# A recurrent attention with a top-2 mixture of experts on one core: products of two units on GpSimd beside the first solve, zeros and copies on other engines, gathers placed one by one

## The chip, the core and the metric

One core of a Trainium2 chip runs the whole program. The metric is the device time of one execution in microseconds (us); the median of the runs counts. The engines are TensorE (PE, with its weight loads PEld), VectorE (DVE), ScalarE (ACT), GpSimd (POOL) and SyncE (SP, which issues most DMAs). All run side by side, each takes its own instructions in order, and they wait for each other by semaphores.

## What is computed

```python
for t in range(S):                      # batch 4, 8 heads, S = 768, head size 40
    y[:, :, t] = einsum('bhd,bhde->bhe', rt, state)
    Sa = einsum('bhde,bhe->bhd', state, at)
    state = state*wt - outer(Sa, bt) + outer(vt, kt)
x = y as 3072 rows of 320
noisy = x @ w_gate + log1p(exp(x @ w_noise)) * noise      # 8 experts
top2, weights = softmax over the two largest
out[row] += weight * (relu(x[row] @ w1[e]) @ w2[e])       # for both experts of a row
```

## The kernel before

The recurrence is cut into 24 units of 64 steps (`NU`, `C`). A unit needs decays (a logarithm, a running sum by matmul, two exponentials), products of a and kb with these decays, a triangular 64x64 system for each of 32 heads, and then a chain of matmuls that carries the state on. `run` writes the order of every engine out by hand, iteration n for unit n, with the decays and products of unit n+8 (`LP`) prepared on the way. The systems of four units are solved together: `xtr` transposes the lower triangles into one tile X, `solve` or (first group only) `solve16` eliminates step by step on DVE (two TENSOR_TENSORs a step, L662 and L663), and `tout` or `tout16` transposes the result back.

Ahead of the loop stands `ramp` (L812), which prepares units 0 to 7, sets all constants, and ends in `first` (L854), the chain of unit 0. The names that matter, with their lines:

- `ln`, `sm`, `ex` (L585 to L599): the decays of unit u: a logarithm on ACT, four matmuls on PE, then on ACT a square with its accumulator read (`lc`) and two exponentials, into the tiles wq and B. `gc` (L826) copies the last decays, 104x8 numbers, to the tile gam by a DVE copy.
- `aprod`, `kprod` (L604, L607): three TENSOR_TENSORs that multiply a and kb by the decays; on POOL unless an engine is given. In `ramp` units 0 to 3 run on DVE ahead of the solve; in `first` units 4 to 7 run on DVE behind it (`vprods`).
- `LS`, `LSd` (L613, L624): 32 matmuls of the products of one unit, the ACT copy of their result into the tile la, and two small ACT copies.
- `xtr(0)` (L628), `xmask16` (L647, two DVE memsets), `solve16` (L657), `tout16` (L664: three DVE transposes and two DVE memsets of 32x512).
- `consts1(i)` (L546): constants in parts, most of them POOL memsets; part 3 also writes four identities of 32x1024 on ACT (L564). `consts16` (L652): three ACT copies of identities and a scaled copy of la, which `S16a` reads.
- `S16a`, `S16b` (L672, L678): the second stage of the first solve (PE, then ACT); `TA`, `TB`, `U`, `UT`, `P`, `Y`: the chain of a unit, each PE and then ACT, DVE in `P` and `Y`. `KBT`, `AK`, `W1`, `W2`: what stands beside it.
- `warm` (L568): matmuls of zeros whose only use is activity on PE; 24 of them (`WR`) stand before the solve's result is needed.

PE, ACT, DVE, POOL and SP each take these in the order in which `ramp` and `first` write them, so an instruction that waits holds back all behind it on its engine.

The experts follow. Rows of one expert are fetched by `gather` (L308), one indirect DMA on POOL's queue for each 128 rows, through lists that SP loads (`lists`, L303), and results go back by indirect DMAs that add (`add`, L377). Part 0 of an expert is its first 384 rows (three gathers), part 1 the next 448 (four). `experts` (L428) issues part 1 of experts 0 and 1 as soon as the lists are there, and `rest` (L437) both parts of expert 2; here a planner orders the instructions by its own costs. `s.after(i, e)` ties instruction i behind e; the list p holds instructions (relus of the hidden blocks, scalings of output tiles) that `rest` uses as such places.

Of the kernel before, what the change touches and what calls it, by code (L numbers as in the profile page):

```python
# [13 lines left out]
ALU = mybir.AluOpType  # L14
# [38 lines left out]
class Moe:  # L53
# [266 lines left out]
    def trans(s,x,e,X=None,part=0):  # L320

# [6 lines left out]
    def after(s,i,e): s.tc.add_manual_dep(i.ins,e.ins.name,mybir.DependencyInfo(mybir.DependencyClass.Sync,mybir.DependencyReason.DATA),reason="place")  # L328
# [166 lines left out]
class Att:  # L495
# [50 lines left out]
    def consts1(s,i):  # L546
        nc=s.nc; G=nc.gpsimd
        if i==0:
            G.memset(s.mk32,1.0)
            for q in range(4): G.affine_select(out=s.mk32[32*q:32*q+32,0],in_=s.mk32[32*q:32*q+32,0],pattern=[[-1,32]],base=0,channel_multiplier=1,compare_op=ALU.is_gt,fill=0.0)  # L550
        if i==1:
            s.m.ident(); G.memset(s.mk,1.0)
            for b in range(2): G.affine_select(out=s.mk[64*b:64*b+64,0],in_=s.mk[64*b:64*b+64,0],pattern=[[1,64]],base=0,channel_multiplier=-1,compare_op=ALU.is_gt,fill=0.0)
            for q in range(4): G.tensor_copy(s.i32[32*q:32*q+32],s.m.idm[32*q:32*q+32,32*q:32*q+32])
        if i==2:
            for z in s.kt: G.memset(z,0.0)
            G.memset(s.fl(s.d1)[:,128:512],0.0)
            for z in s.w: G.memset(z,0.0)
            G.memset(s.iw,0.0)
        if i==3:  # L560
            for b in range(2):
                for z,o,c in ((s.dg,32,32),(s.rp,0,0)):
                    q=slice(64*b+o,64*b+o+32)
                    nc.scalar.activation(z[q,:,c:c+32],s.m.idm[q,q].rearrange("p (o x)->p o x",o=1).to_broadcast([32,32,32]),AF.Copy)  # L564
            for z in s.S+s.St: G.memset(z,0.0)
    def warm0(s,pp,k):
        for _ in range(k): s.nc.tensor.matmul(pp,s.wz,s.wz[:,0:1].to_broadcast([128,512]),start=True,stop=True)
    def warm(s,pp,k):  # L568
        z=s.fl(s.d1)
        for _ in range(k): s.nc.tensor.matmul(pp,z[:,0:128],z[:,0:512],start=True,stop=True)  # L570
# [86 lines left out]
    def solve16(s):  # L657
        V=s.nc.vector; X=s.X; ap=lambda o,*d: bass.AP(X.tensor,X.offset+o,[X.ap[0],[528,2],*d])
        for j in range(1,15):
            m=15-j  # L660
            t=s.wk.tile([128,240],F32,name="Tt",bufs=1)[:,:2*j*m].rearrange("p (b k i)->p b k i",b=2,i=m); x=ap(j+1,[32,j],[1,m])
            V.tensor_tensor(t,ap(33*j+1,[0,j],[1,m]),ap(j,[32,j],[0,m]),op=ALU.mult)  # L662
            s.hs=V.tensor_tensor(x,x,t,op=ALU.add)  # L663
    def tout16(s):  # L664
        V=s.nc.vector; X=s.X
        V.transpose(s.rp[:,:,32:64].rearrange("p k t->p t k"),X.rearrange("p s t->p t s"))
        V.transpose(s.d16[:,:,0:16].rearrange("p k s->p s k"),X[:,0:16])
        V.transpose(s.dg[:,:,16:32].rearrange("p k s->p s k"),X[:,16:32])
# [143 lines left out]
    def ramp(s):  # L812
        nc,m=s.nc,s.m; V,G=nc.vector,nc.gpsimd
        s.consts(); s.ea=None; H=s.lh
        def load(u):
            H('ga',s.a,u); H('gkb',s.kb,u)
# [9 lines left out]
        def gc(u): V.tensor_copy(s.gam[0:RF,u],s.B[u%2][0:RF,0:520].rearrange('p (j c)->p j c',c=65)[:,:,0])  # L826
# [278 lines left out]
```

## Time and profile before

| | us |
|---|---|
| runs shown | 812.16, 810.92, 804.20 |
| their median | 810.92 |
| the profiled execution | 805.83 |
| its span, first to last instruction | 804.0 |
| busy in the span: PE, DVE, ACT, POOL | 728.4, 501.4, 399.6, 339.3 |

What lies outside the span is 1.83 us. Views of one execution give the start of an instruction from the span's start, its length, its engine and line, and in brackets how long the engine had been idle and what ended that. Several instructions of a kind are merged into a row, with xN.

### The profile page before, as it was taken

To read this page: it belongs to the slowest core of one execution; us is meant where nothing else is said; L and a number is where in the kernel's file an instruction comes from. 1 tells how busy PE (TensorE), PEld (TensorE's weight loads), DVE (VectorE), ACT (ScalarE), POOL (GpSimd) and SP (SyncE) were. 2 spreads that over 40 slices of the span, in tenths; PEclk is the share of its full clock that TensorE was granted. 3 is DMA by queue.
4 is the path that set the end of the run, shared out by engine and by line. 5 is a ranking of instruction groups with operands and counts; after the bars stand their busy time and mean duration, and the time that the engine had idled before them with its cause. 6 is when DMAs were issued, how large, how long until landed. Compare 5 with 4: busy or idle time off the path is not lost.

```text
span 804.0 us, 29172 instructions
## 1 busy us (share of the span) xinstructions
PE 728.4 (91%) x12632; PEld 531.1 (66%) x12632; DVE 501.4 (62%) x1069; ACT 399.6 (50%) x873; POOL 339.3 (42%) x463
## 2 busy tenths in 40 slices
PE   6588899999989899898888798999999999999994
PEld 4377778888877777677654365657566665766662
DVE  7866667777989857845464476856565664652321
ACT  6566667677666453464431245544434534442220
POOL 9702243345377544344358515425435151513223
PEclk9779999999999999999999899999999999999998
DMA  6542345554544632352307535536445162402113
GB/s 203 175 103 69 110 134 154 152 155 148 157 141 136 181 93 74 102 158 85 110 2 172 133 85 144 115 112 128 124 110 143 27 139 87 49 5 32 23 20 39
DMA packets 67700, 87.07 MB, mean 108 GB/s; under 512 B 15640, under 2 KB 52460, under 8 KB 67564
## 3 DMA queue, kind: packets, MB, share of 16 engines
q1 hardware_dynamic: 55404, 67.98, 28.6%
q0 software_dynamic: 12160, 17.15, 12.4%
q8 instruction: 101, 1.65, 0.9%
q14 instruction: 35, 0.29, 0.1%
HBM read 63.41 MB, written 21.69 MB: 106 GB/s over the span
## 4 chain that ended last, share of the span: by engine, by line
PE 71%; DVE 12%; ACT 8%; issue 5%; POOL 2%; DMA 0%; another core or an unknown queue 0%; ACTq 0%; DVEq 0%; POOLq 0%
PE po L369 22%; PE ph L354 20%; PE py L786 3%; PE pp L770 3%; PE pt L334 2%; PE rl L801 2%; PE tb L701 2%; PE ta L691 2%; ACT la L524 2%; ACT dr L524 2%; PE sm L591 1%; DVE Tt L640 1%; PE ut L749 1%; PE pw L723 1%; PE pw L732 1%
## 5 line engine op out<-in xcount | busy, mean ns | idle before, releaser
L377 POOL DMA_INDIRECT out_dram<-y,le x45 | 74.6, 1658 | 192.5 <-ACT y L371 189.8
L354 PE MATMUL ph<-rw__68,rk 128*128 128x384 f16 (+1 forms) x512 | 97.0, 339 | 2.9 <-DVE hl L356 1.8
L354 PE MATMUL ph<-dr,la 128*128 128x448 f16 (+1 forms) x384 | 86.0, 339 | 3.0 <-issue 3.0
L369 PEld LDWEIGHTS <-rk 128*128 128x128 f16 x576 | 56.7, 100 | 36.6 <-issue 6.6
L354 PEld LDWEIGHTS <-rk 128*128 128x128 f16 x512 | 49.5, 98 | 39.4 <-issue 3.3
L371 ACT ACTIVATE y<-po,le 128x320 f32<-128x320 f32 (+1 forms) x53 | 26.6, 504 | 93.1 <-PE po L369 79.7
L182 POOL DMA_INDIRECT ls<-ent,po x48 | 50.5, 1052 | 52.9 <-ACT pm L524 31.8
L356 DVE SCALAR_TENSOR_TENSOR hl<-ph,hh 128x448 f16<-128x448 f32 x64 | 39.2, 622 | 46.0 <-ACT hh L355 45.8
L355 ACT ACTIVATE hh<-ph 128x448 f16<-128x448 f32 x64 | 34.1, 541 | 66.0 <-PE ph L354 65.9
L355 ACT ACTIVATE rk<-ph 128x384 f16<-128x384 f32 x64 | 30.9, 488 | 62.1 <-PE ph L354 43.6
L369 PEld LDWEIGHTS <-hh 128*128 128x128 f16 (+1 forms) x640 | 46.5, 103 | 18.5 <-issue 2.7
L242 DVE TENSOR_REDUCE yc<-y 128x1 f32<-128x320 f32 (+1 forms) x53 | 23.8, 456 | 55.0 <-ACT y L371 54.9
L640 DVE TENSOR_TENSOR Tt<-X__71 128x30 f32<-128x30 f32 (+9 forms) x150 | 55.7, 372 | 3.7
L354 PEld LDWEIGHTS <-la 128*128 128x128 f16 x384 | 37.2, 98 | 29.2 <-issue 3.7
L356 DVE SCALAR_TENSOR_TENSOR rk<-ph,rk 128x384 f16<-128x384 f32 x64 | 34.4, 552 | 33.7 <-ACT rk L355 24.2
L612 POOL TENSOR_TENSOR rk<-rk,B 104x512 f32<-104x512 f32 x30 | 35.5, 1183 | 42.3 <-DVE lg L805 41.3
L641 DVE TENSOR_TENSOR X__71<-X__71,Tt 128x30 f32<-128x30 f32 (+9 forms) x150 | 49.8, 332 | 5.5
L369 PE MATMUL po<-ra,rk 128*128 128x320 f16 x288 | 45.7, 305 | 2.9 <-ACT rk L355 2.4
L786 PE MATMUL py<-pm,kt 128*64 128x104 f32 (+1 forms) x768 | 40.5, 254 | 4.1 <-issue 2.7
L772 DVE TENSOR_TENSOR pm<-pp,mk 128x1024 f32<-128x1024 f32 x24 | 29.4, 1223 | 16.5 <-PE pp L770 15.8
L786 PEld LDWEIGHTS py<-pm,kt 128*64 128x64 f32 x768 | 34.7, 137 | 7.4 <-issue 4.3
L369 PE MATMUL po<-w2h,rk 128*128 128x320 f16 x192 | 34.5, 308 | 4.3 <-issue 3.1
(329 smaller groups left out, 1731.3 us busy)
## 6 DMA issues: line engine op xcount, KB each, us to landing
rk<-in_gkb_dram SPq DMA_DIRECT2D x48, 160.0 KB
w2r<-in_w_dram SPq DMA_DIRECT2D x6, 1280.0 KB
w1s<-in_w_dram SPq DMA_DIRECT2D x28, 256.0 KB
xd<-xr SPq DMA_DIRECT2D x40, 160.0 KB
w1s<-in_w_dram SPq DMA_DIRECT2D x5, 1024.0 KB
out_dram<-z SPq DMA_DIRECT2D x15, 320.0 KB
rw__68<-in_gw_dram SPq DMA_DIRECT2D x24, 160.0 KB
ra<-in_ga_dram SPq DMA_DIRECT2D x48, 80.0 KB
```

Of the source, the lines that this page charges most:

```text
L182: st=nc.gpsimd.indirect_dma_start(out=s.ls,out_offset=OFFS(ap=po[:,j,k:k+1],axis=0),in_=s.ent[:,j,k],in_offset=None)
L354: for i,(a,b) in enumerate(mm): s.hmm=nc.tensor.matmul(ph[:,:n],a,b,start=i==0,stop=i==7)
L355: s.hrelu=nc.scalar.activation(hh[:,f],ph[:,:n],AF.Relu)
L356: s.hhl=nc.vector.scalar_tensor_tensor(hl[:,f],ph[:,:n],0.0,hh[:,f],op0=ALU.max,op1=ALU.subtract)
L369: for j in range(c): nc.tensor.matmul(po[p*j:p*j+p,:d],h[:,f,r],w[:,f,d*j:d*j+d],start=k==0,stop=k==23)
L377: st=s.nc.gpsimd.indirect_dma_start(out=o[0],out_offset=OFFS(ap=o[1],axis=0),in_=o[2],in_offset=None,compute_op=ALU.add)
L524: s.ea=s.nc.scalar.activation(*a,**k)
L612: s.after((eng or s.nc.gpsimd).tensor_tensor(z,z,b1,op=ALU.mult),e)
L640: eng.tensor_tensor(t,X[:,j:j+1,j+1:].to_broadcast([128,j,m]),X[:,0:j,j:j+1].to_broadcast([128,j,m]),op=ALU.mult)
L641: s.hs=eng.tensor_tensor(X[:,0:j,j+1:],X[:,0:j,j+1:],t,op=ALU.add)
L772: nc.vector.tensor_tensor(m.rearrange("p y j x->p (y j) x")[...,0:64],pp.rearrange("p y (j t)->p (y j) t",t=64),s.mk.to_broadcast([128,16, ...
L786: nc.tensor.matmul(pp[64*y:64*y+64,b,128*hh:128*hh+n],kt[:,j,y],m[:,y,j,0:n],start=first and hh==0,stop=True,skip_group_check=True)
```

## The change

Units 4 and 5 get their products (and the copy to gam) on POOL right after their decays and ahead of `solve16`, units 6 and 7 stay on DVE behind it; `LS(4)`, `LSd(4)`, `ex(6)`, `ln(7)`, `sm(7)`, and the matmuls of `LS(5)` move ahead of the solve, and the chain in `first` is written in another order. The loads of units 5 and 6 and the zeros of the tile kt come earlier, the zeros of S, St, w and iw later. On DVE the copy to gam becomes a TENSOR_TENSOR max, and the memsets of `xmask16` become TENSOR_TENSORs of zeros. Zeros of d1 (which `warm` reads) and of dg move to ACT. `warm` runs 8 matmuls instead of 24, and 6 more are tied behind step 8 of `solve16`. In the experts the gathers of part 1 of expert 1 and of both parts of expert 2 are tied one by one to places in p.

```diff
-    def loadx(s,e,X=None,part=0):
+    def loadx(s,e,X=None,part=0,places=()):
-        s.lists(e,X,part)
-        for _ in s.gather(e,X,part): pass
+        s.lists(e,X,part); places=list(places)
+        for g in s.gather(e,X,part):
+            if places: s.after(g,places.pop(0))
...
-        r2=s.load2(1); s.loadx(0,x,1); s.loadx(1,xn,1); ll=s.hlist.ins
+        r2=s.load2(1); s.loadx(0,x,1); s.lists(1,xn,1); ll=s.hlist.ins
...
         s.trans(x[0],0,X,1); hx=s.hx3.ins; H1=s.hidden(W1,X,1,p); s.after(s.piece1(2,5),p[5])
+        for k,g in enumerate(s.gather(1,xn,1)): s.after(g,p[3+k])
...
-              xn=s.loadx(e+1); s.loadx(e+1,xn,1); ...
+              xn=s.loadx(e+1,places=p[7:10] if e==1 else ()); s.loadx(e+1,xn,1,p[10:] if e==1 else ()); ...
...
-FT,FS,FL,FU,WR,W0,WU=2,2,4,2,24,5,2
+FT,FS,FL,FU,WR,W0,WU,WJ,WQ=2,2,4,2,8,5,2,8,6
...
+    def null16(s): s.nc.scalar.activation(s.fl(s.d1)[:,128:512],s.z[:,0:1].to_broadcast([128,384]),AF.Copy)
...
-        V=s.nc.vector; V.memset(s.X[:,0:16,16:32],0.0); V.memset(s.fl(s.X)[:,0:1024:33],1.0)
+        ... V.tensor_tensor(s.X[:,0:16,16:32],z,z,op=ALU.mult); z=s.z[:,0:32]; V.tensor_tensor(s.fl(s.X)[:,0:1024:33],z,z,op=ALU.is_equal)
...
-        for b in range(2): V.memset(s.dg[64*b+32:64*b+64,:,16:32],0.0)
+        for b in range(2): s.nc.scalar.activation(s.dg[64*b+32:64*b+64,:,16:32],s.z[...]...,AF.Copy)
...
-        def gc(u): V.tensor_copy(s.gam[0:RF,u],s.B[u%2]...[:,:,0])
+        def gc(u): z=s.B[u%2]...[:,:,0]; V.tensor_tensor(s.gam[0:RF,u],z,z,op=ALU.max)
...
-        LS[3](); s.LSd(3); s.lmask(3); s.ex(4); s.ln(5); s.sm(5); gc(4); s.ex(5); s.xtr(0); gc(5)
-        s.consts1(2); gn(6); s.consts1(3); s.xmask16()
-        s.ea=None; s.lv(0); loads(5)
+        LS[3](); s.LSd(3); s.lmask(3); s.ex(4); s.ln(5); s.sm(5); s.xtr(0); s.ex(5); s.ln(6); s.sm(6)
+        def gp(u): s.aprod(u); s.kprod(u,1); s.kprod(u,0); G.tensor_copy(s.gam[0:RF,u],...)
+        gp(4); s.xmask16(); gp(5); s.KBT(0)(); s.ex(6); s.ln(7); s.consts1(3); s.consts16()
+        s.ea=None; s.lv(0)
+        a4=s.LS(4); s.W1(0); s.warm(s.p1t('wm'),WR); a4(); s.LSd(4); s.sm(7,s.p2('sm')); s.a5=s.LS(5)
...
-        gn(7,8)
+        gn(7); s.consts1(4); gn(8)
...
-        s.KBT(0)(); s.consts16(); s.ln(6); s.W1(0)
-        s.warm(s.p1t("wm"),WR)
-        s.sm(6,s.p2("sm"))
...
-        s.solve16(); s.hA=s.hs; s.tout16(); s.first()
+        s.solve16(); s.hA=s.hs
+        if WQ: s.after(s.warm(s.p1t("wm"),WQ),s.h8)
+        s.tout16(); s.first()
...
-        s.vprods(4); s.vprods(5)
-        s.S16a(0); s.S16b(0); a4=s.LS(4); s.W2(0); s.ex(6); s.TA(0); a4(); s.ln(7); a5=s.LS(5); s.TB(0); s.vprods(6)
-        s.sm(7); a5(); s.U(0); s.LSd(4); k=s.KBT(1); s.UT(0); s.ex(7)
-        a6=s.LS(6); s.LSd(5); k(); s.ln(LP)
-        s.P(0); s.vprods(7); s.S16a(1); a6(); s.LSd(6); s.AK(1); s.Y(0); a7=s.LS(7); s.S16b(1); s.sm(LP); a7(); s.LSd(7); s.ex(LP)
+        s.S16a(0); s.vprods(6); s.gcp(6); s.a5(); s.LSd(5); s.S16b(0); s.ex(7); s.vprods(7); s.gcp(7)
+        s.W2(0); s.TA(0); k=s.KBT(1); s.TB(0); a6=s.LS(6)
+        s.U(0); k(); s.ln(LP); s.UT(0); a6(); s.LSd(6); a7=s.LS(7)
+        s.P(0); s.S16a(1); a7(); s.LSd(7); s.AK(1); s.sm(LP); s.Y(0); s.ex(LP); s.S16b(1)
```

## Rows read from the trace of the kernel before

**Rows 1.** The chain that ended last, 0 to 64 us: start, us, what.

```profile
21.52 8.44 DVE gam L826
```

**Rows 2.** Timeline of DVE: start, us, engine, line, operation, out<-in, form.

```profile
6.03 0.69 DVE L606 TENSOR_TENSOR ra<-ra,rw__68 104x512 f32<-104x512 f32 x1 [1.31 <-ACT rw__68 L524]
...
21.60 8.36 DVE L630 STREAM_TRANSPOSE X__71<-la 128x1024 f32<-128x1024 f32 x1
...
31.34 0.23 DVE L662 TENSOR_TENSOR Tt<-X__71 128x72 f32<-128x72 f32 x1
...
37.92 0.21 DVE L663 TENSOR_TENSOR X__71<-X__71,Tt 128x28 f32<-128x28 f32 x1
...
42.35 1.11 DVE L669 MEMSET dr<- 32x512 f32 x2 [0.16 <-DMA rb<-in_grb_dram]
...
73.69 0.75 DVE L640 TENSOR_TENSOR Tt<-X__71 128x30 f32<-128x30 f32 x1
...
125.41 0.18 DVE L640 TENSOR_TENSOR Tt<-X__71 128x30 f32<-128x30 f32 x1
```

**Rows 3.** Timeline of POOL around the same times.

```profile
5.53 0.96 POOL L540 MEMSET rk<- 128x1024 f32 x1
...
21.30 0.94 POOL L818 MEMSET rk<- 128x1024 f32 x1
...
29.73 0.20 POOL L81 MEMSET tri<- 128x128 f16 x1
30.00 0.29 POOL L82 TENSOR_SCALAR_AFFINE_SELECT tri<-tri 128x128 f16<-128x128 f16 x1
...
73.20 1.19 POOL L606 TENSOR_TENSOR ra<-ra,rw__68 104x512 f32<-104x512 f32 x1
```

**Rows 4.** Timeline of POOL and DVE at 252.4 to 253.3 us.

```profile
252.48 0.73 POOL L798 TENSOR_TENSOR S<-S,gam 128x320 f32<-128x320 f32 x1 [0.86 <-DVE l L216]
...
252.95 0.28 DVE L220 TENSOR_TENSOR wq<-l 128x4 f32<-128x4 f32 x1
...
253.17 1.18 POOL L606 TENSOR_TENSOR ra<-ra,rw__68 104x512 f32<-104x512 f32 x1
```

**Rows 5.** Timeline of ACT.

```profile
25.18 4.25 ACT L564 ACTIVATE dr<-idm 32x1024 f32<-32x1024 f32 x4
...
30.16 1.46 ACT L655 ACTIVATE w1s<-w1s 128x512 f32<-128x512 f32 x3
...
41.67 0.28 ACT L524 ACTIVATE w1s<-sa 128x128 f32<-128x128 f32 x1 [8.24 <-PE sa L676]
...
63.94 0.70 ACT L524 ACTIVATE dr<-sb 128x128 f32<-128x128 f32 x3 [4.08 <-PE sb L683]
...
65.30 0.84 ACT L524 ACTIVATE la<-la 32x256 f32<-32x256 f32 x2
...
69.38 0.76 ACT L524 ACTIVATE dr<-ta 32x256 f32<-32x256 f32 x2
```

**Rows 6.** Timeline of PE: the matmuls of `warm`.

```profile
25.99 5.35 PE L570 MATMUL wm<-d 128*128 128x512 f16 x24
```

**Rows 7.** Busy ACT in three stretches that hold ex(6), LS(4), ln(7) and LSd(4).

```profile
sum 3.47, ACT 3.40; mean ACT 1.13
```

**Rows 8.** Busy time by stretch: us, PE, PEld, DVE, ACT, POOL (instructions), granted clock, DMA share.

```profile
38.20:49.00 10.80, 7.10 (x263) 5.90 (x267) 10.43 (x14) 3.92 (x12) 0.31 (x1) 0.50 0.64 135
...
436.00:441.00 5.00, 5.00 (x39) 3.60 (x38) 4.21 (x4) 0.00 (x0) 3.78 (x5) 1.00 0.71 223
441.00:446.40 5.40, 2.26 (x11) 0.82 (x9) 0.48 (x1) 0.53 (x1) 3.15 (x4) 0.86 0.35 106
446.40:452.00 5.60, 5.60 (x22) 3.15 (x21) 0.70 (x2) 1.05 (x2) 2.61 (x2) 0.52 0.75 145
```

**Rows 9.** Timeline of POOL: first and last of ten gathers.

```profile
431.94 1.01 POOL L313 DMA_INDIRECT rk<-xd,le  x1 [0.33 <-DMA le<-ls]
...
443.24 0.95 POOL L313 DMA_INDIRECT rk<-xd,le  x1 [0.30 <-issue]
```

More of the change, by code (lines that the diff above doesn't have):

```diff
@@ L449, in rest @@
               r1=s.load1(e+1) if e>1 else s.w1s
-              xn=s.loadx(e+1); s.loadx(e+1,xn,1); r2=s.load2(e+1) if e>1 else s.r2
+              xn=s.loadx(e+1,places=p[7:10] if e==1 else ()); s.loadx(e+1,xn,1,p[10:] if e==1 else ()); r2=s.load2(e+1) if e>1 else s.r2
             if e>1: H0=s.hidden(W1,X,0)
@@ L555, in consts1 @@
         if i==2:
-            for z in s.kt: G.memset(z,0.0)
-            G.memset(s.fl(s.d1)[:,128:512],0.0)
+            pass
+        if i==4:
+            for z in s.S+s.St: G.memset(z,0.0)
             for z in s.w: G.memset(z,0.0)
@@ L564, in consts1 @@
                     nc.scalar.activation(z[q,:,c:c+32],s.m.idm[q,q].rearrange("p (o x)->p o x",o=1).to_broadcast([32,32,32]),AF.Copy)
-            for z in s.S+s.St: G.memset(z,0.0)
+            s.null16()
+    def null16(s): s.nc.scalar.activation(s.fl(s.d1)[:,128:512],s.z[:,0:1].to_broadcast([128,384]),AF.Copy)
     def warm0(s,pp,k):
@@ L569, in warm @@
         z=s.fl(s.d1)
-        for _ in range(k): s.nc.tensor.matmul(pp,z[:,0:128],z[:,0:512],start=True,stop=True)
+        o=[s.nc.tensor.matmul(pp,z[:,0:128],z[:,0:512],start=True,stop=True) for _ in range(k)]
+        return o[0] if o else None
     def fl(s,z): return z.rearrange("p a b->p (a b)")
@@ L598, in ex, with gcp @@
         s.act(B[:,:,0:64],z,AF.Exp)
-        if u>5: s.nc.gpsimd.tensor_copy(s.gam[0:RF,u],B[0:RF,:,0])
+        if u>=LP: s.gcp(u)
+    def gcp(s,u): s.nc.gpsimd.tensor_copy(s.gam[0:RF,u],s.B[u%2][0:RF,0:520].rearrange('p (j c)->p j c',c=65)[:,:,0])
     def scans(s,u):
@@ L647, in xmask16 @@
     def xmask16(s):
-        V=s.nc.vector; V.memset(s.X[:,0:16,16:32],0.0); V.memset(s.fl(s.X)[:,0:1024:33],1.0)
+        V=s.nc.vector; z=s.z[:,0:1].rearrange('p (o x)->p o x',o=1).to_broadcast([128,16,16]); V.tensor_tensor(s.X[:,0:16,16:32],z,z,op=ALU.mult); z=s.z[:,0:32]; V.tensor_tensor(s.fl(s.X)[:,0:1024:33],z,z,op=ALU.is_equal)
     def lmask(s,u):
@@ L663, in solve16 @@
             s.hs=V.tensor_tensor(x,x,t,op=ALU.add)
+            if j==WJ: s.h8=s.hs
     def tout16(s):
@@ L668, in tout16 @@
         V.transpose(s.dg[:,:,16:32].rearrange("p k s->p s k"),X[:,16:32])
-        for b in range(2): V.memset(s.dg[64*b+32:64*b+64,:,16:32],0.0)
+        for b in range(2): s.nc.scalar.activation(s.dg[64*b+32:64*b+64,:,16:32],s.z[64*b+32:64*b+64,0:1].rearrange('p (o x)->p o x',o=1).to_broadcast([32,32,16]),AF.Copy)
     def S16(s,u):
@@ L825, in vp, with gc @@
         def vp(u): s.aprod(u,V); s.kprod(u,1,None,V); s.kprod(u,0,None,V); gc(u)
-        def gc(u): V.tensor_copy(s.gam[0:RF,u],s.B[u%2][0:RF,0:520].rearrange('p (j c)->p j c',c=65)[:,:,0])
+        def gc(u): z=s.B[u%2][0:RF,0:520].rearrange('p (j c)->p j c',c=65)[:,:,0]; V.tensor_tensor(s.gam[0:RF,u],z,z,op=ALU.max)
         f=s.p2("wm")[:,0]
@@ L831, in ramp, with gp @@
         LS[0]=s.LS(0); vp(1); s.ln(3); s.sm(3); s.Sq[3]=s.Sp; LS[0](); s.LSd(0); s.consts1(1); G.memset(s.dg,0.0); s.warm0(f,WU)
-        ex(2); s.lcv(3); LS[1]=s.LS(1); vp(2); s.lmask(0); ex(3); LS[1](); s.LSd(1); gn(5); G.memset(s.rp,0.0); s.warm0(f,WU)
+        ex(2); s.lcv(3); LS[1]=s.LS(1); vp(2); s.lmask(0); ex(3); LS[1](); s.LSd(1); gn(5); loads(5); G.memset(s.rp,0.0); gn(6); loads(6); [G.memset(z,0.0) for z in s.kt]; s.warm0(f,WU)
         LS[2]=s.LS(2); V.tensor_reduce(s.m16,s.i32[:,16:32],axis=AX.X,op=ALU.add); vp(3); s.lmask(1); s.ln(4); LS[2](); s.LSd(2); s.warm0(f,WU); LS[3]=s.LS(3); s.AK(0); s.sm(4); s.lmask(2)
-        LS[3](); s.LSd(3); s.lmask(3); s.ex(4); s.ln(5); s.sm(5); gc(4); s.ex(5); s.xtr(0); gc(5)
-        s.consts1(2); gn(6); s.consts1(3); s.xmask16()
-        s.ea=None; s.lv(0); loads(5)
+        LS[3](); s.LSd(3); s.lmask(3); s.ex(4); s.ln(5); s.sm(5); s.xtr(0); s.ex(5); s.ln(6); s.sm(6)
+        def gp(u): s.aprod(u); s.kprod(u,1); s.kprod(u,0); G.tensor_copy(s.gam[0:RF,u],s.B[u%2][0:RF,0:520].rearrange("p (j c)->p j c",c=65)[:,:,0])
+        gp(4); s.xmask16(); gp(5); s.KBT(0)(); s.ex(6); s.ln(7); s.consts1(3); s.consts16()
+        s.ea=None; s.lv(0)
+        a4=s.LS(4); s.W1(0); s.warm(s.p1t('wm'),WR); a4(); s.LSd(4); s.sm(7,s.p2('sm')); s.a5=s.LS(5)
         for z in s.vt+s.r[:1]+s.rb[:1]: G.memset(z,0.0)
-        gn(7,8)
+        gn(7); s.consts1(4); gn(8)
         for z in s.r[1:]+s.rb[1:]: G.memset(z,0.0)
@@ L841, in ramp @@
         m.consts2(s.z)
-        s.KBT(0)(); s.consts16(); s.ln(6); s.W1(0)
-        s.warm(s.p1t("wm"),WR)
-        s.sm(6,s.p2("sm"))
-        s.ea=None; H('gv',s.vt,0); H('gr',s.r,0); H('grb',s.rb,0); s.lv(1); loads(6); load(7); load(8)
+        s.ea=None; H('gv',s.vt,0); H('gr',s.r,0); H('grb',s.rb,0); s.lv(1); load(7); s.lw(9); load(8)
         for y in range(2): nc.sync.dma_start(s.iw[64*y:64*y+40].rearrange("p h x->p (h x)"),s.A['iw'][y])
         s.vc(0); m.marks()
-        s.lw(LP+1); load(LP+1); H('gr',s.r,1); H('grb',s.rb,1); s.lv(2); s.lw(LP+2)
+        load(LP+1); H('gr',s.r,1); H('grb',s.rb,1); s.lv(2); s.lw(LP+2)
         m.consts3(); m.consts4()
         for i in range(ZR): m.zero(i,ZP)
-        s.solve16(); s.hA=s.hs; s.tout16(); s.first()
+        s.solve16(); s.hA=s.hs
+        if WQ: s.after(s.warm(s.p1t("wm"),WQ),s.h8)
+        s.tout16(); s.first()
     def vprods(s,u):
```

## The prediction

> **What bounds the kernel now.** The page comes first: PE is busy in 728.4 of 804.0 us, so little can be won by making an engine faster, and what counts is where the chain leaves PE. The chain of waits shows that at the start of the program: its longest single piece is a DVE copy of 104x8 numbers that took 8.44 us, from 21.52 to 29.96 [rows 1]. The timeline of DVE shows why that matters: the transpose xtr(0) behind it lasts 8.36 us by the record and ends at the same moment, and the first solve, all of it DVE, follows and ends at 38.13 [rows 2]. The timeline of POOL tells what stood against the copy: memsets back to back from 21.30 on, each issued before the one ahead was over, until a hole of 0.07 us at 29.93 (the memset of tri ends, the select starts at 30.00) [rows 3]. The copy ends 0.03 us later. So a DVE copy and a POOL memset exclude each other, and a dense row of memsets can keep the copy out.
>
> A DVE TENSOR_TENSOR isn't kept out by a memset: at 6.03 one took 0.69 us inside a POOL memset of 5.53 to 6.49 [rows 2, 3]. By a POOL TENSOR_TENSOR it is: at 73.69 a solve step of 30 numbers took 0.75 us instead of 0.18 and ended 0.05 us behind POOL's product [rows 2, 3].
>
> After the solve the bound is ACT: it sat idle for 8.24 us up to 41.67, waiting for PE and so for the solve, and then works through unit 0 until the copy of TA(1) ends at 70.14 [rows 5]. That end, where the loop's pace takes over, is my mark: what it moves I count for the whole run, as all later units hang on it.
>
> **The solve.** The new gam copies and the zeros of X are TENSOR_TENSORs, so memsets no longer hold DVE. Against that stand the POOL products of units 4 and 5: six at 1.19 us and two small copies [rows 3], 7.5 us together, starting at about 21.1, when the decays of unit 4 come (the copy at 21.52 waited for the last of them). xtr(0) runs beside them; three transposes in a row take 4.06 us (38.13 to 42.19, the end of the wait before the memset at 42.35) [rows 2], so one is some 1.4 to 2, ending near 22.3. The DVE steps then find POOL busy. At a border between two POOL products one DVE step slips through: one of 4 numbers issued at 252.95 ended at 253.23, just past the product ahead (253.21), though POOL's next had been issued at 253.17 [rows 4]. So until POOL is done DVE gets one step per POOL instruction: the two of xmask16 and about four of the solve's 28. Adding some 0.9 us for these to POOL's 7.5 brings POOL's end to 29.5. The other 24 steps took 6.8 us before (31.34 to 38.13) [rows 2], with memsets beside them as now: the solve ends at 36.3, 1.8 us earlier. Bounds: without any blocking, 22.3 + 0.6 + 7.7 = 30.6; if DVE is kept out for all of POOL's row, 28.7 + 0.6 + 7.7 = 37.0.
>
> The Trainium skill speaks against this part: "SBUF — State Buffer", section "Who interferes with whom", says that a VectorE instruction with two SBUF inputs contends with a GpSimd instruction that reads SBUF, and that whoever issues first holds the shared ports for that whole instruction. The row at 73.69 agrees, but the copy of 8.44 us waited through some fifteen memsets, not for one. By the page's rule the solve ends at 36.3, by the copy's row at 37.0; the page changes the sum by 0.7 us.
>
> **What stands before S16a.** That the solve is earlier doesn't yet help, as ACT and PE have more ahead of it. ACT now does ex(6), ln(7) and the kt copy first, until about 30.8 (their matmuls start at 25.6, when ACT is through with unit 5; I add the PE and ACT times one by one). Then come the identities, 4.25, null16 at about 0.45, so 35.5; consts16 with its la copy, 2.2 (1.46 and about 0.7), LS(4), LSd(4) and vc(0), about 2.4: ACT is free at 40.0 [rows 5]. The zeros of dg, two ACT writes of 32x512, must wait for the last transpose, 36.3 + 4.06 = 40.4. The trace lacks that form: 32x256 took 0.42 each, 32x1024 1.06 [rows 5]; between them I take 0.63, so 41.65. The DVE memsets that go cost 1.11 [rows 2], off this path.
>
> On PE the 8 matmuls of warm wait for null16, 35.5, because they read its zeros. 24 took 5.35 [rows 6], 0.22 each; PE has idled for some 6 us by then, and after the like idle before 40.56 it ran at the low level (granted clock 0.50 from 38.2 to 49.0) [rows 8], so up to twice that. Warm 1.8 to 3.6, sm(7) 1.2 to 2.1, LS(5) 0.7 to 1.2, the 6 further warm matmuls 1.3 to 2.6, S16a 0.7 to 1.1: S16a ends between 41.2 and 46.1. I take 43.0 for the start of its copy on ACT, nearer the fast end, since dense matmuls run first; it was 41.67. So here the kernel is 1.3 us late, not early.
>
> **The chain of unit 0.** From that copy to the end of TA(1)'s took 28.47 us (41.67 to 70.14) [rows 5]. Two things leave it. ACT's work for ex(6), LS(4), ln(7) and LSd(4), 3.40 us [rows 7], now lies in the idle 8.24 ahead. And LS(7)'s copy, LSd(7) and ex(8), about 3.2 (0.6, 0.84, 1.8), which stood behind ACT's wait of 4.08 for S16b [rows 5], now come before it, while PE runs Y(0). 28.47 - 3.40 - 3.2 = 21.9. DVE loses the products of units 4 and 5 there; ACT's chain hides those anyhow. TA(1) ends at 43.0 + 21.9 = 64.9, 5.2 us earlier. To this I add 0.8 for clock: PE's 7.10 us of work at the low level [rows 8] would take half at the high one, 3.5 less, but most lies off ACT's chain. Sum of the ramp: -6.0. Bounds: 41.7 + 21.9 - 2.7 (the rest of the clock) is -9.2; 46.3 + 25.1 (only the 3.40 leave) is +1.3.
>
> **Moved loads and zeros.** The loads of units 5 and 6 come earlier on SP, ahead of the loads of v, r and vt, which nobody reads before 40. POOL's zeros of S, St, w, and kt end before their readers too; consts2 moves from 35.8 to some 45, and delays SP's list and zero DMAs, read by nobody for 200 us. Cost 0; if w's zeros were late, W2 would wait, by at most the 3 us of that group.
>
> **The gathers.** Ten gathers went out back to back from 431.94 to 444.2 [rows 9]. In 441.0 to 446.4 PE was busy 2.26 of 5.40 us, with nothing to wait for by the profile, and then worked 5.6 us at clock 0.52 [rows 8]: 3.1 + 2.7 = 5.8 us at stake. Against the gathers as cause: from 436 to 441 they ran just so and PE was busy throughout [rows 8]. Bounds 0 and -5.8, and above nothing if a held gather, in order on POOL, keeps an output's add or its own reader waiting, +2. The mechanism isn't shown, so I take -1.0.
>
> **The sum.** 805.83 - 6.0 - 1.0 = 798.8 for an execution like the profiled one, which lies 5.1 below the median of the runs shown, 810.92; from that the sum gives 803.9. The four executions mean 808.3, giving 801.3. I forecast 802.6. About 1%, 8.1 us, is what a measurement of this kernel can tell from no change, and my gain of 7 lies just under it.
>
> **Rivals.**
> - The gathers were the cause of PE's holes: all 5.8 come back, 11.8 in sum, 797.8 by the forecast's level. For it: the holes end with the gathers. Against: 436 to 441. Chance 0.22.
> - The ramp gives little: DVE is kept out for all of POOL's row and PE is cold up to S16a (copy at 45), so 45 + 21.9 = 66.9, a gain of 3.2 that PE's next hole may halve: 807. Chance 0.18.
> - Slower: PE's order. Warm, sm(7), LS(5) and the 6 matmuls stand in front of S16a and all hang on null16, behind ACT's identities. If null16 ends 3 us later, at 38.5, and PE is cold, S16a's copy starts at 49.3; with the stretch at 25.1, TA(1) ends at 74.4: +4.3, about 814. It decides once the copy starts later than 70.14 - 25.1 = 45.0. Against it: ACT has no wait in that time beyond unit 6's matmuls. Chance 0.08.
> - The forecast, 0.52; a third of it, and the first rival, pass 1%.
>
> Faster by over 1%: 0.17 + 0.22 + 0.01 = 0.40. Slower by over 1%: 0.04. Within: 0.56. The range, 795 to 811, holds the forecast's bounds at either level of the runs, the first rival's value and the second's.
>
> **What would show it.** Right: no DVE copy of several us; about six DVE steps of over 1 us beside POOL's products between 21 and 30, and a solve that ends near 36; S16a's copy near 43 behind the two zeros of dg; TA(1)'s copy ending near 65; the holes at 441 to 446 mostly still there. Wrong: a solve ending near 31, S16a's copy after 45, TA(1) after 68, or PE full and at clock 1.00 around the first adds of the experts.

## The result, and the profile after

| | us |
|---|---|
| kernel after: runs | 800.72, 802.98, 802.50, 795.64 |
| their median; before, beside it (4 runs) | 801.61; 811.54 |
| ratio, 95% interval | 0.9887 [0.9845, 0.9929] |
| profiled execution, its span | 800.72, 798.9 |

The time came out 1.0 us from the forecast of 802.6, and faster by 1.1%. The runs say that this sum was right with terms that were not: the ramp gave about half of its 6 us, and the gathers, as worked out below, far more than their 1 us in this job (a job is a set of runs made together on one chip).

The timeline of VectorE in the kernel after; the copy of 8.44 us [rows 1] has no successor, and the transpose that lasted 8.36 us [rows 2] takes 1.96:

```profile
20.57 1.96 DVE L636 STREAM_TRANSPOSE X__71<-la 128x1024 f32<-128x1024 f32 x1
22.56 1.53 DVE L654 TENSOR_TENSOR X__71<-z 128x256 f32<-128x256 f32 x2
23.99 0.17 DVE L668 TENSOR_TENSOR Tt<-X__71 128x28 f32<-128x28 f32 x1
24.20 1.05 DVE L669 TENSOR_TENSOR X__71<-X__71,Tt 128x28 f32<-128x28 f32 x1
25.29 0.21 DVE L668 TENSOR_TENSOR Tt<-X__71 128x52 f32<-128x52 f32 x1
25.53 1.07 DVE L669 TENSOR_TENSOR X__71<-X__71,Tt 128x52 f32<-128x52 f32 x1
...
34.98 0.21 DVE L669 TENSOR_TENSOR X__71<-X__71,Tt 128x28 f32<-128x28 f32 x1
```

The timeline of GpSimd beside it, which answers to [rows 3]:

```profile
21.46 1.18 POOL L612 TENSOR_TENSOR ra<-ra,rw__68 104x512 f32<-104x512 f32 x1
22.60 2.61 POOL L618 TENSOR_TENSOR rk<-rk,B 104x512 f32<-104x512 f32 x2
25.16 0.18 POOL L842 COPY gam<-B 104x8 f32<-104x8 f32 x1
25.31 1.23 POOL L612 TENSOR_TENSOR ra<-ra,rw__68 104x512 f32<-104x512 f32 x1
26.50 2.30 POOL L618 TENSOR_TENSOR rk<-rk,B 104x512 f32<-104x512 f32 x2
```

Steps of 0.2 us last over 1 us here, each until just past the end of a GpSimd product; at 23.99 and 25.29 a short one goes through as well. From 28.93 on they are short, and the solve ends at 35.19 (38.13 before [rows 2]).

The timeline of ScalarE, to be read against [rows 5]:

```profile
31.83 4.25 ACT L567 ACTIVATE dr<-idm 32x1024 f32<-32x1024 f32 x4
36.09 0.52 ACT L569 ACTIVATE d<-z 128x384 f16<-128x384 f32 x1
...
40.91 1.26 ACT L676 ACTIVATE dr<-z 32x512 f32<-32x512 f32 x2
43.76 0.28 ACT L526 ACTIVATE w1s<-sa 128x128 f32<-128x128 f32 x1 [1.58 <-PE sa L683]
...
62.53 0.60 ACT L526 ACTIVATE rw__68<-sm 128x512 f32<-128x512 f32 x1 [3.48 <-PE sm L596]
...
65.84 0.70 ACT L526 ACTIVATE dr<-sb 128x128 f32<-128x128 f32 x3 [2.23 <-PE sb L690]
...
68.24 0.76 ACT L526 ACTIVATE dr<-ta 32x256 f32<-32x256 f32 x2
```

TA(1)'s copy ends at 69.00, where 64.9 was forecast and before had 70.14. What stands in its way shows in the chain that ended last, at 56.6 to 64.9 us:

```profile
56.77 0.62 PE ak L717 x30
57.38 2.72 issue
60.10 0.33 PE ak L717 x2
60.43 2.00 PE sm L596 x8
62.43 2.24 PE py L793 x32
```

TensorE stops in the middle of a group with nothing to wait for, and then runs at the lower level of its clock. So one of the prediction's signs of being wrong, TA(1) after 68, was met.

In the experts the picture is reversed. Busy time by stretch, the same three as the last of [rows 8]:

```profile
436.00:441.00 5.00, 5.00 (x39) 3.60 (x37) 4.78 (x6) 0.53 (x1) 3.78 (x5) 1.00 0.92 287
441.00:446.40 5.40, 5.40 (x37) 3.54 (x36) 1.97 (x4) 2.14 (x4) 3.26 (x3) 1.00 0.72 126
446.40:452.00 5.60, 4.42 (x24) 2.28 (x22) 3.74 (x6) 1.37 (x3) 3.52 (x3) 1.00 0.73 162
```

and the timeline of GpSimd, gathers and adds, to be read against [rows 9]:

```profile
434.99 1.02 POOL L313 DMA_INDIRECT rk<-xd,le  x1 [2.07 <-DMA le<-ls]
...
438.85 0.91 POOL L313 DMA_INDIRECT rk<-xd,le  x1 [0.30 <-issue]
440.07 1.61 POOL L378 DMA_INDIRECT out_dram<-y,le  x1 [0.30 <-issue]
...
445.17 1.01 POOL L313 DMA_INDIRECT rw__68<-xd,le  x1 [0.30 <-issue]
```

TensorE is full at clock 1.00 where before it was busy 2.26 of 5.40 us: another sign that the prediction had named as "wrong". Set side by side by TensorE's groups, the trace of after stands level with before at unit 5, is 1.45 us behind at 410 us, 7.3 ahead at 452 and 5.1 ahead at the end.

### The profile page after: what moved, and what is told of

It is laid out like the page before. It is cut to its first block, busy times and chain, and to the rows that moved or that the text cites. A ratio compares the mean times of both kernels' runs of the same rounds, so it can differ in the third digit from the quotient of the medians.

```text
span 798.9 us, 29160 instructions
## 1 busy us (share of the span) xinstructions
PE 728.6 (91%) x12622; PEld 532.5 (67%) x12622; DVE 495.0 (62%) x1059; ACT 401.9 (50%) x876; POOL 348.7 (44%) x470
## 4 chain that ended last, share of the span: by engine, by line
PE 74%; ACT 9%; DVE 8%; issue 4%; DMA 2%; another core or an unknown queue 1%; POOL 1%; SPq 0%; ACTq 0%; DVEq 0%; POOLq 0%
PE po L370 21%; PE ph L355 20%; PE py L793 4%; PE pp L777 4%; PE rl L808 2%; PE pt L335 2%; PE sm L596 2%; PE tb L708 2%; ACT la L526 2%; PE ta L698 2%; PE kt L722 2%; ACT dr L526 2%; PE pw L739 2%; ACT tt L526 1%; PE pw L730 1%
## 5 line engine op out<-in xcount | busy, mean ns | idle before, releaser
L618 POOL TENSOR_TENSOR rk<-rk,B 104x512 f32<-104x512 f32 x34 | 40.4, 1191 | 42.8 <-DVE lg L812 41.3
L793 PE MATMUL py<-pm,kt 128*64 128x104 f32 (+1 forms) x768 | 43.5, 261 | 6.1 <-issue 4.6
L793 PEld LDWEIGHTS py<-pm,kt 128*64 128x64 f32 x768 | 36.7, 142 | 10.5 <-issue 7.4
L313 POOL DMA_INDIRECT rk<-xd,le x28 | 28.1, 1005 | 24.5 <-ACT hh L356 6.7
```

The lines of the kernel that those rows point to most:

```text
L618: s.after((eng or s.nc.gpsimd).tensor_tensor(z,z,b1,op=ALU.mult),e)
L793: nc.tensor.matmul(pp[64*y:64*y+64,b,128*hh:128*hh+n],kt[:,j,y],m[:,y,j,0:n],start=first and hh==0,stop=True,skip_group_check=True)
```

## The experiments

The kernel before took 784.6, 785.9 and 787.4 us beside three of the later jobs and 810.7 beside the fourth, so ratios are compared, and absolute times only within a job. What differs between a job of 785 to 787 us and one of 811 us isn't known; the job of 787.4 us and that of 810.7 us bear the same chip number, 1, so the number doesn't tell them apart. The marks of all profiles stand here once: end of the first solve, start of the copy behind S16a, end of TA(1)'s and TA(5)'s copies (us from the span's start), and the stretch from the end of attention's last read-out (rl) to the start of the first transposes (pt) behind the first two outputs of the experts.

| kernel | ratio [95%] | solve | S16a | TA(1) | TA(5) | stretch |
|---|---|---|---|---|---|---|
| before | 1 | 38.13 | 41.67 | 70.14 | 130.69 | 53.70 |
| after | 0.9887 [0.9845, 0.9929] | 35.19 | 43.76 | 69.00 | 130.71 | 45.31 |
| e1 gathers | 1.0000 [0.9974, 1.0026] | 38.68 | 42.22 | 71.48 | 132.77 | 40.91 |
| g1 gathers | 0.9991 [0.9964, 1.0018] | 38.67 | 42.21 | 70.45 | 130.00 | 40.91 |
| e2 ramp | 0.9972 [0.9949, 0.9996] | 35.25 | 44.03 | 66.64 | 125.02 | 41.00 |
| g2 ramp | 0.9953 [0.9928, 0.9978] | 35.06 | 43.34 | 68.61 | 128.94 | 40.99 |
| f0 after | 0.9974 [0.9947, 1.0000] | 35.28 | 43.42 | 68.46 | 129.13 | 40.91 |
| e3 zeros | 0.9985 [0.9951, 1.0020] | 36.02 | 45.84 | 69.71 | 130.92 | 40.92 |
| e4 copies | 0.9941 [0.9914, 0.9967] | 33.17 | 36.73 | 67.18 | 130.29 | 40.99 |
| g3 copies | 0.9935 [0.9907, 0.9963] | 33.05 | 36.61 | 66.50 | 126.15 | 40.99 |
| f1 warm | 1.0004 [0.9981, 1.0028] | 33.10 | 36.34 | 66.53 | 132.04 | 40.97 |
| f2 both | 1.0005 [0.9983, 1.0027] | 33.54 | 36.78 | 66.63 | 129.22 | 40.91 |
| f3 zeros first | 0.9961 [0.9938, 0.9984] | 35.63 | 44.06 | 69.52 | 131.99 | 40.91 |
| h1 copies, gathers | 0.9845 [0.9808, 0.9883] | 32.12 | 35.33 | 64.85 | 124.72 | 46.16 |

**The gathers alone (e1, g1).** The hunks of `loadx`, `experts` and `rest`, on the kernel before:

```diff
-        r2=s.load2(1); s.loadx(0,x,1); s.loadx(1,xn,1); ll=s.hlist.ins
+        r2=s.load2(1); s.loadx(0,x,1); s.lists(1,xn,1); ll=s.hlist.ins
...
+        for k,g in enumerate(s.gather(1,xn,1)): s.after(g,p[3+k])
...
```

> The kernel before, with the placing of the gathers alone; the ramp is that of before. Theory A (the gathers carry the gain; in the two traces after goes from 1.45 us behind at 410 us to 7.3 us ahead at 452 us and ends 5.1 us ahead): 804 to 806 us where before takes about 811.5 us, and no idle of TensorE over 0.4 us without a named releaser between 436 and 447 us. Theory B (the ramp carries it, as I forecast, and the gathers are worth about 1 us): 810 to 811 us, with the holes between 441 and 447 us still there.

> The kernel of e1_gathers again, to have it on the chip of this run beside the two next. Theory H (the gathers help only where TensorE is held in the experts): where before takes about 811 us, a ratio of 0.990 to 0.994; where it takes about 785 us, 0.997 to 1.003 as in e1. Rival: they are worth nothing on a slower chip either, 0.998 to 1.002.

Measured: 784.13 us where before took 784.61, and 786.24 where it took 787.44. Neither job had the 811 us for which theories A and B gave their times, so these runs don't decide between them; theory H gave 0.997 to 1.003 for such a job, and that came. The stretch is 40.91 us with the gathers placed, in e1, g1, f0, f2 and f3, and 40.97 to 41.00 without, in e2, g2, e4, g3 and f1: here the placing is worth 0.1 us. There are no holes for it to fill: the stretch, 53.70 us in the trace of before, takes 41 with the gathers of before too.

**The ramp alone (e2, g2),** the kernel after with those hunks undone.

> The kernel after, with the gathers put back as before had them; only the ramp differs from before. Theory A (the ramp is worth nothing by unit 5, where the two traces stood at the same time): 810 to 813 us, holes of TensorE in the experts as in before. Theory B (the ramp is worth the 6 us forecast): 804 to 806 us. In both the copy behind S16a lands near 43.8 us and that of TA(1) near 69 us, as in after.

> The kernel of e2_ramp again, on the same chip as g1. Theory H: a ratio of 0.996 to 0.999 on either kind of chip (e2 had 0.9972), so that on a slower chip g1 and g2 together come to the 0.989 of the change. Rival: the ramp carries the change on a slower chip, 0.988 to 0.991, and g1 is at 1.

Measured: 3.2 and 4.9 us below the medians of before, 2.2 and 3.7 us by the ratios. So the ramp is worth 2 to 4 us in these jobs, neither nothing nor 6. g2's 0.9953 lies just under the 0.996 to 0.999 expected. No run has the ramp alone where before takes 811 us.

**The whole change elsewhere (f0).**

> The kernel after, unchanged, beside many runs of before on the chip of this run. Theory H (the gathers are worth something only where TensorE is held in the experts without a named reason, as in the traces of 800 us and more; the ramp is worth 2 to 3 us): where before takes about 785 us, 781 to 783 us, a ratio of 0.995 to 0.998, and no holes over 0.4 us between 425 and 450 us in this kernel; where before takes about 811 us, a ratio of 0.985 to 0.993. Rival I (the change is worth the same 10 us everywhere): a ratio of 0.987 to 0.990 on either.

Measured: 0.9974, theory H's value for such a job; rival I fell. The change is worth 1.1% in the first job and a quarter of a per cent here. What sets the two kinds of job apart lies in the second half of attention and in the stretch: from the 12th read-out to the 24th the traces of before, after and h1, all from jobs of 811 us, take 167.8, 168.7 and 168.0 us, all others 154.6 to 161.8, whatever the kernel.

**Copies and gathers, without the new order (h1).** The edit of e4 (below) and that of e1 together. In this job before takes 811 us.

> The kernel before with the decay copies as a max (e4_copies) and the gathers placed as after has them: the two parts of the change that can be had without the new order of the ramp. Theory: where before takes 784 to 788 us the gathers add nothing, a ratio of 0.992 to 0.996, under the 0.9974 of f0_after; where before takes about 811 us, 0.980 to 0.988. The stretch from the last read-out of attention to the first transposes of the experts' rows takes 42.2 to 42.5 us, as in every other run of this study whether the gathers are placed or not. Rival: the two work against each other, 0.997 or more.

Measured: 797.48 us where before took 810.66, in the range that theory gave for such a job. The expected 42.2 to 42.5 us for the stretch (reckoned there to the end of the transposes, 1.4 us more than in the table) missed: by the table it is 46.16, where after has 45.31 and before 53.70. What is special in such a job shows in the timeline of TensorE in h1, at TA(22):

```profile
360.03 0.26 PE L693 MATMUL ta<-dr,la 32*32 32x32 f32 x4
360.75 0.22 PE L693 MATMUL ta<-dr,la 32*32 32x32 f32 x2 [0.46 <-issue]
361.47 0.23 PE L693 MATMUL ta<-dr,la 32*32 32x32 f32 x2 [0.50 <-issue]
362.20 0.29 PE L693 MATMUL ta<-dr,la 32*32 32x32 f32 x6 [0.49 <-issue]
```

and the same 32 matmuls in the timeline of f0:

```profile
359.97 0.69 PE L698 MATMUL ta<-dr,la 32*32 32x32 f32 x32
```

TensorE is let go in steps of 0.72 us, with some 0.5 of each lost, and no row names a reason. The timeline of TensorE in before has such holes too:

```profile
429.72 0.65 PE L354 MATMUL ph<-dr,la 128*128 128x384 f16 x3 [1.42 <-issue]
...
432.08 0.65 PE L354 MATMUL ph<-dr,la 128*128 128x384 f16 x3 [0.90 <-issue]
...
441.44 0.30 PE L369 MATMUL po<-w2h,rk 128*128 128x320 f16 x1
442.85 0.57 PE L369 MATMUL po<-w2h,rk 128*128 128x320 f16 x3 [1.11 <-issue]
444.27 0.30 PE L369 MATMUL po<-w2h,rk 128*128 128x320 f16 x1 [0.86 <-issue]
444.99 0.71 PE L369 MATMUL po<-w2h,rk 128*128 128x320 f16 x2 [0.42 <-issue]
446.40 0.96 PE L369 MATMUL po<-w2h,rk 128*128 128x320 f16 x3 [0.70 <-issue]
```

From 441.44 on they are on the same raster, steps of 1.41, 1.42, 0.72 and 1.41, and the first two open at 428.30 and 431.18, ahead of the first of the ten gathers at 431.94 [rows 9]. So the gathers don't make that hold, which is there in attention too, but in the two traces with the gathers spread the stretch loses about 8 us less to it. By the ratios it is the same: 0.9887 over the ramp's mean of 0.9963 is 0.992, 0.9845 over the copies' 0.9938 is 0.991, 6 to 8 us of 811, with some 4 us either way by the intervals. This is worked out across jobs, and not shown: the gathers alone, the ramp alone and the copies alone never ran in such a job, and only one trace of before shows the stretch at 53.70, so that a ramp worth more there, or a hold that was longer by chance in that execution, stay rivals. What holds TensorE stays open.

**One line of the ramp (e4, g3).** Only the form of the decay copies, on the kernel before:

```diff
-        def gc(u): V.tensor_copy(s.gam[0:RF,u],s.B[u%2][0:RF,0:520].rearrange('p (j c)->p j c',c=65)[:,:,0])
+        def gc(u): z=s.B[u%2][0:RF,0:520].rearrange('p (j c)->p j c',c=65)[:,:,0]; V.tensor_tensor(s.gam[0:RF,u],z,z,op=ALU.max)
```

> The kernel before, with one edit: the decay copies of the ramp are a TENSOR_TENSOR max of the tile with itself in place of a copy; the order, the zeros and the gathers are those of before. Theory E (the copy of 8.44 us was kept out by the form of the copy beside a GpSimd that zeroes without a break, and the solve behind it holds the ramp): the copy takes 0.2 to 1.5 us, the solve ends at 30 to 32 us where before ends at 38.13, the copy behind S16a at 36 to 39 us, and the total is 806 to 809 us. Rival F (another wait takes its place: zeros or transposes that the solve or S16a needs, or clock and code on TensorE later): the solve is earlier, but the total is 810 to 813 us. Rival G: the max is kept out as the copy was, 8 us, and nothing changes.

> The kernel of e4_copies again (only the decay copies written as a max). Theory J (the earlier solve is worth 3 to 5 us by itself, and the six warming matmuls of f1_warm cost it): a ratio of 0.992 to 0.996. Rival N (e4's 0.9941 was its chip, and the earlier solve goes to low clock and code reads): 0.998 to 1.002, as f1_warm.

The timeline of VectorE in e4:

```profile
21.18 0.17 DVE L826 TENSOR_TENSOR gam<-B 104x8 f32<-104x8 f32 x1 [1.28 <-ACT B L524]
21.27 1.95 DVE L630 STREAM_TRANSPOSE X__71<-la 128x1024 f32<-128x1024 f32 x1
```

and that of GpSimd beside it, two of a row of memsets that goes on to 30.61, as in before:

```profile
21.15 0.41 POOL L559 MEMSET iw<- 128x384 f32 x1
21.51 0.52 POOL L818 MEMSET ra<- 128x512 f32 x1
```

0.17 us in place of 8.44; e1, with the old form, has 8.59. The solve ends at 33.17 (30 to 32 expected), S16a's copy comes 5 us earlier than in before, and the ratios, 0.9941 and 0.9935, agree. So one line gives about what the whole new ramp does, which has that line too (0.9972 and 0.9953; the intervals overlap, and in the job of g2 and g3 the two medians are 782.67 and 782.56).

**Warming matmuls (f1, f2).** e4 with the six that after holds to the solve's step 8 (the 24 of before stay); f2 with the gathers too.

```diff
...
-        s.solve16(); s.hA=s.hs; s.tout16(); s.first()
+        s.solve16(); s.hA=s.hs
+        s.after(s.warm(s.p1t("wm"),WQ),s.h8)
+        s.tout16(); s.first()
```

> The kernel before with the decay copies as a max, as e4_copies, and six warming matmuls held to the solve's step 8, as after has them. Theory J (in e4 TensorE's clock was at the lower level from 35.1 to 48.7 us, over S16a and the first TA, and that is what eats the earlier solve): the clock is full from about 40 us, the copy behind TA(0) ends 1 to 3 us before 43.9 us, and the ratio to before is 0.990 to 0.993 where e4 had 0.9941. Rival K (the clock falls again a few us later, or the six stand in front of S16a): the first marks move, the total stays at 0.994.

> f1_warm with the placing of the gathers as after has it. Theory H: where before takes about 785 us the same as f1_warm within 1.5 us; where before takes about 811 us, 5 to 7 us less than f1_warm. Rival: the gathers cost or save 3 us or more on either.

The clock did what was meant: the lower level began at 39.7 us in f1, and S16a ran at the full one (0.72 us, in e4 1.05). The copy behind TA(0) ended at 43.88 and 44.42, not earlier than e4's 43.92, and the total is 1.000: theory J and rival K both miss: e4's gain isn't there. The gathers change nothing here (f2 within 1.5 us of f1, as theory H has it). The single profiles show 23.9 us at the lower level between 36 and 130 us for f1 and 13.7 for f2, much as the 23.0 of e4 and the 15.4 of g3, so the clock doesn't tell them apart. So the six seem to cost 0.6%; but e4's kernel wasn't run in the job of f1 and f2, so this too is worked out across jobs, and a cause stays open.

**ScalarE's zeros (f3).** On the kernel after:

```diff
-            s.null16()
...
+... [G.memset(z,0.0) for z in s.kt]; G.memset(s.fl(s.d1)[:,128:512],0.0); s.warm0(f,WU)
...
-        for b in range(2): s.nc.scalar.activation(s.dg[64*b+32:64*b+64,:,16:32],s.z[64*b+32:64*b+64,0:1].rearrange('p (o x)->p o x',o=1).to_broadcast([32,32,16]),AF.Copy)
+        for b in range(2): V.memset(s.dg[64*b+32:64*b+64,:,16:32],0.0)
```

> The kernel after, with two of its zeros taken from ScalarE: that of the warming operand is a GpSimd memset behind those of the kt tiles, and those of dg behind the solve are VectorE memsets as before had them. Theory L (ScalarE's zero at 36.09 us, behind the identities, puts the warming matmuls, the decay sums of unit 7 and so S16a late; this is the 2 us by which S16a's copy is later than in before): S16a's copy starts at 40 to 41.5 us where after has 43.76, the copy behind TA(1) 2 to 3 us earlier, and the total is 2 to 3 us under that of f0_after. Rival M (what the ramp gains goes to low clock and code reads on TensorE before unit 5): S16a's copy is earlier, the total within 1 us of f0_after.

Both theories miss S16a: its copy stays at 44.06. The timeline of TensorE tells why:

```profile
30.75 1.90 PE L573 MATMUL wm<-d 128*128 128x512 f16 x8
32.49 1.06 PE L595 MATMUL sm<-TR,L 128*128 128x128 f32 x8
39.28 1.25 PE L624 MATMUL ls<-rk,ra 64*64 64x64 f32 x32 [5.73 <-POOL cumh L84]
40.46 2.74 PE L573 MATMUL wm<-d 128*128 128x512 f16 x6
43.13 0.87 PE L682 MATMUL sa<-dr,w1s 32*32 32x16 f32 x64
```

The first eight come six us earlier and unit 7's sums seven and a half, and then LS(5) waits. The view names a GpSimd memset of 38.72, but ScalarE's copy of LS(4), whose PSUM pool LS(5) shares, ends at 39.17. That copy stands behind the identities and consts16, 6.3 us of ScalarE from 32.36 on. So ScalarE's queue holds LS(5), by whichever of its instructions comes last. Behind LS(5) and in front of S16a stand the six warming matmuls, 2.74 us at the lower level here; S16a starts as they end, 2 us after the last zeros of dg (41.07). TensorE's order, the prediction's rival for a slower kernel, is the other half of the hold; the kernel after without the six wasn't run. The total, 0.9961, isn't told from f0's, as rival M has it.

**Zeros of the output (e3).** On the kernel after:

```diff
-ZN,ZP,ZR=2,16,4
+ZN,ZP,ZR=2,16,0
```

> The kernel after, with ZR 0 in place of 4: no zeros of the output are written in the ramp, all are spread over the later units. Theory C (TensorE's hole of 2.72 us at 57.38 us is its next code waiting behind the zeros, which fill the DMA engines from 55 to 58 us): the hole goes, the code is read near 55 us, the copy behind TA(1) ends near 66.3 us, and the total is 798 to 800.5 us where after takes 801.6. Rival D (the hole belongs to the code's place, or to the clock): a hole of 2 to 3 us stays between 56 and 61 us and the total is that of after, 801 to 803 us.

Busy time by stretch (granted clock, DMA share and GB/s last) in after:

```profile
55.00:58.00 3.00, 2.38 (x147) 2.03 (x138) 1.22 (x1) 2.12 (x6) 0.00 (x0) 1.00 1.01 276
58.00:61.00 3.00, 0.90 (x5) 0.83 (x6) 0.53 (x1) 1.01 (x4) 0.00 (x0) 0.89 0.06 14
```

and in e3:

```profile
55.00:58.00 3.00, 2.43 (x64) 2.05 (x68) 0.00 (x0) 2.95 (x8) 0.00 (x0) 0.84 0.00 0
58.00:61.00 3.00, 3.00 (x141) 2.85 (x134) 1.23 (x1) 1.47 (x4) 0.00 (x0) 0.50 0.03 5
```

The hole is gone, as theory C has it, but the rest of it missed: the code is read at 58.60, TA(1) ends at 69.71, and the ratio is 0.9985 (after, in another job, 0.9974). S16a's copy comes 2.1 us later in this execution than in after, and TensorE runs at the lower level from 57.1 to 63.9, 6.8 us where after has 3.4 there, so that this pair alone doesn't say what took the hole away. What it is was then shown by accident. In e3 the zeros of xd go out at 316.86, and the DMA engines are full (share 0.99) from 319 to 324. The timeline of TensorE there:

```profile
322.70 0.68 PE L747 MATMUL u<-w,tt 64*64 64x64 f32 x29 [0.34 <-ACT tt L526]
326.36 0.33 PE L747 MATMUL u<-w,tt 64*64 64x64 f32 x3 [2.98 <-issue]
```

A hole of the same size, at another place. What both have in common is in the DMA records of one queue, which the third part of after's page lists with packets, MB and share:

```profile
q8 instruction: 101, 1.65, 0.9%
```

That is 16.3 KB a read, one for each 256 or so of TensorE's 25,000 instructions. In after no read starts between 52.03 and 57.90 us, while TensorE goes through 391 instructions; the one at 57.90 begins as the zeros end, and TensorE resumes at 60.10. In e3 the same: 391 instructions, a read at 324.06, and TensorE again 2.3 us behind it. From TensorE's instruction no. 1474 to the start of the next read pass 2.62 us in after, 2.29 in f0, 1.75 in g2 and 2.79 in f3, at a DMA share of 0.95 or more; where the engines are idle, 0.60 in e3 and 1.12, 0.74 and 0.78 in before, e1 and g1. So it is the full engines that keep the read waiting. Counted with the weight loads, the holes of f0 (1.64 us), g2 (0.76) and f3 (3.31) stand before the same instruction as after's, no. 1730, and the others of 0.35 us or more without a releaser from 45 to 130 us at 1474, 1985, 2753, 3009, 3778, 4033, 4545 and 5313: 256 apart or a multiple of it, but for one or two; a single one, 0.80 us in h1, lies elsewhere. Before has them too, 1.81 us at 61.78 and 1.44 at 95.24.

## Why the prediction was right in sum and wrong in its parts

- **The copy of 8.44 us, and a max that memsets don't keep out:** right, by e4's 0.17 us.
- **"The solve ends at 36.3":** 35.06 to 35.28 in four traces of that ramp. One number was off in all, GpSimd wasn't lengthened by the 0.9 us added (its row ends at 28.95 in after and 28.52 in f0, not 29.5); the other, about four of the solve's steps beside that row, held in f0, where after had six. The contention is real: from the start of xtr(0) to the solve's end after needs 14.62 us, e4 11.90, so GpSimd's row of six products and two copies costs 2.7 us of the path. The rule of the Trainium skill, "SBUF — State Buffer", section "Who interferes with whom", that had been weighed here agrees: each long step ends 0.04 to 0.1 us behind a GpSimd product.
- **"I take 43.0 for the start of S16a's copy":** 43.76, and right in its mechanism. The two zeros of dg took 1.26 us, the estimate of 0.63 each; they began at 40.91 for 40.4.
- **"28.47 - 3.40 - 3.2 = 21.9":** this step failed. The stretch took 25.24 us, 3.3 more. The two subtractions are in the trace (ex(6), LS(4), LS(7) and their copies are where they were put), but from 54.45 to 65.82 TensorE, not ScalarE, bounds the stretch: a hole of 2.72 us and the lower clock on unit 8's sums and Y(0) lie on the chain. sm and py took 2.00 and 2.24 us there, 1.09 and 1.58 at the full level in before: 1.57 more. Taking both out leaves 21.0, but that this is near 21.9 is partly luck: the 28.47 held a hole of its own (1.81 us at 61.78), which the step carried over unseen, and low clock too (up to 48.97). So 0.9 of the 3.3 is the longer hole and 1.6 the place of the lower level; the rest isn't told apart. The 0.8 us counted as a gain from the clock didn't come: the stretch has 6.8 us at the lower level, before had 7.3.
- **The ramp, -6.0:** mis-sized by half. Over the four traces with that ramp and the gathers' places of either kernel (after, f0, e2, g2) TA(1) ends at 68.18 on average, over the three with the old ramp (before, e1, g1) at 70.69: 2.5 us. That the mark carries to the end fits here, on average: at TA(5) the difference is 2.7, in time 2.2 and 3.7 us. As a rule it fails: f1 and f2 have TA(1) at 66.5 and 66.6, 4 us ahead of the old ramp, and no gain, and TA(5) differs by 5.7 us between traces of the new ramp.
- **Moved zero DMAs, "cost 0":** wrong in its reason. Nobody reads those zeros for 200 us, but they came some 5 us later than before and filled the DMA engines just when TensorE's next code was due. What that costs in the whole isn't shown: e3, without the output's zeros in the ramp, has 0.9985.
- **The gathers, -1.0:** about 0.1 us in three jobs and, worked out but not shown, -6 to -8 where TensorE is held. The first rival had this size, with 5.8 us, though not the cause: two of the holes come before the ten gathers. The argument against it, that TensorE was busy from 436 to 441 with the gathers running, doesn't bear on a hold that comes and goes by itself and that the gathers may only lengthen.

The two errors, 3 us too much and 5 to 7 too little, left the gain, 7.0, 3 us short of the 9.9 between the medians; and the level from which it was taken, 802.6 + 7.0 = 809.6, lay 1.9 us under before's 811.54. That the time came within 1.0 us is luck.

## What to carry to other kernels

Where an engine is kept out by another's stream of short instructions, try the form of that one instruction before a new order: one line gave 0.6%, the rebuilt ramp with it 0.3 to 0.5. Bulk writes that nobody reads can still stop TensorE where a fast stretch of small matmuls needs its code; look for holes of TensorE with no releaser beside a DMA share of 1. A hole that no row explains may belong to the job rather than the kernel, so the ratio to a kernel run beside it counts, and in more than one job. h1, faster than before by 1.55% in its job, may be a better version than after (0.9845 to 0.9887, and e4's 0.994 to 0.9974), but the intervals overlap, and only a side-by-side run would settle that.

## What the runs showed of the hardware

- TensorE stops for 0.4 to 3.3 us where its next 16 KB of code have not come, and goes on 2.2 to 2.6 us after the read begins (after, f0, g2, f3; 2.3 in e3); the read waits while the DMA engines are full. The same place cost 2.72, 1.64, 3.31 and 0.76 us in four executions, and none in e2, where TensorE was at the lower clock (0.51 from 55 to 58 us) and so not yet through its code.
- In some jobs TensorE is let go only in steps of about 0.72 us in parts of attention and the experts, at a granted clock of 1.00; half of attention then takes 168 us for 155 to 162.
- Beside a row of GpSimd products (1.2 to 1.4 us each) a VectorE step of two SBUF inputs gets through at the end of a product, 1.0 to 1.2 us for 0.2, and now and then a short one with it; a dense row of memsets doesn't hold such a step (0.17 us in e4), but kept out a copy for 8.4 and 8.6 us.
- The stretches at the lower clock fall differently in two executions of one program: from 46 us on after has them at 46.7, 60.4 and 80.8 us, f0 at 54.1 and 61.0.
